# Two layers of windowed attention and MLP: K copied to bf16 before it is spread by parity, PV sums divided block by block

## The chip, the cores and the metric

The kernel runs on one core of a Trainium2 chip. The metric is the time of one execution on the device in microseconds; the median of three runs before the change is 485.0 us.

A core has five engines that run side by side, each in its own program order: TensorE (PE, matmul, with a weight load PEld of its own), VectorE (DVE), ScalarE (ACT), GpSimd (POOL) and SyncE (SP, which issues DMAs here). Matmuls write to PSUM, which has 8 banks; this kernel gives 4 of them to the attention scores (one tile of 4 banks) and 4 single ones to everything else.

## The reference

Two layers, each a windowed attention with 32 heads of 16 and a ReLU MLP, each with a normalization ahead of it and a residual sum behind it. The weights of both layers are the same.

```python
def _A_ref(x, wqkv, wo):                     # x: 1 x 2048 x 512, bf16
    B, S, D = x.shape
    H = 32; Dh = D // H; W = 256
    qkv = (x @ wqkv).reshape(B, S, 3, H, Dh).transpose(2, 0, 3, 1, 4)
    q, k, v = qkv[0], qkv[1], qkv[2]
    scores = jnp.einsum("bhqd,bhkd->bhqk", q, k) * (Dh ** -0.5)
    mask = (idx[:, None] - idx[None, :] >= 0) & (idx[:, None] - idx[None, :] < W)
    p = softmax(where(mask, scores, -1e9))
    o = jnp.einsum("bhqk,bhkd->bhqd", p, v)
    return o.transpose(0, 2, 1, 3).reshape(B, S, D) @ wo

def _B_ref(x, w1, w2):                       # w1: 512 x 1792, w2: 1792 x 512
    return jnp.maximum(x @ w1, 0) @ w2

x = A_x
x = x + _A_ref(layernorm(x), A_wqkv, A_wo);  x = x + _B_ref(layernorm(x), B_w1, B_w2)
x = x + _A_ref(layernorm(x), A_wqkv, A_wo);  x = x + _B_ref(layernorm(x), B_w1, B_w2)
```

## The kernel before

The rows are worked in 8 steps: 2 layers of 4 chunks of 512 rows, called k = 0 to 7. The kernel is written as a graph of small operations, each with the engines it may run on, an assumed time for each, the operations it depends on, and the buffers it takes. While the program is built, a list scheduler in Python plays the graph through with those assumed times and records the instructions of each engine in the order that it finds. On the chip that order is fixed; where an assumed time is off, an engine waits. Where the scheduler sees TensorE idle for 0.4 us, it puts a matmul on an identity there ("warm").

The buffers of the shared kind:

```python
    ps_s = ctx.enter_context(tc.tile_pool(name="ps_s", bufs=1, space=bass.MemoryType.PSUM))  # scores, 4 banks
    psum = Pool("p", 4, ps_d)      # 4 single banks: Q, K, V, PV sums, wo, w1, w2, warm
    xns = Pool("xn", 3, work)
    stg = Pool("stg", 3, work)     # V on its way, and the output rows
    ots = Pool("OT", 3, work)
    EVAC = {512: {"DVE": 0.67, "ACT": 0.59}, 256: {"DVE": 0.42, "ACT": 0.38}}   # assumed times
```

K lies in SBUF twice, once for the even and once for the odd heads of a pair of 16 rows, with the rows of the other parity multiplied by zero (`par` holds 1 or 0 for each partition). It is written by VectorE or ScalarE straight from the PSUM bank of K's matmuls. `KBD` is a ring of 20 slots of 64 keys; a chunk that reaches over the end is written in two pieces for each parity.

```python
    def spread_k(e, layer, c, t, h0, h1, ps):
        ...                                   # pieces a to b of the ring
            for p in range(2):
                o = KBD[:, t, sa:sa + b - a, p, :]
                i = ps[:, 64 * a:64 * b].rearrange("p (s k) -> p s k", k=64)
                if e == "ACT":
                    act.activation(o, i, ACT.Copy, scale=par[:, p:p + 1])
                else:
                    dve.tensor_scalar(out=o, in0=i, scalar1=par[:, p:p + 1], scalar2=None, op0=ALU.mult)
```

```python
        # plan_qkv(k), for each of 4 groups t of 8 heads (chunk 0 in two halves h of 256 rows)
                at = first_slot[units_of[k][t + 4 * (h or 0)]] - wait          # wait = 16 score tiles, 0 in chunk 0
                box, m = group(at, KC, us, kmm, ...)                           # K's matmuls in one bank
                times = {"DVE": 1.46, "ACT": 1.42} if h is None else {"DVE": 0.87, "ACT": 0.83}
                k_done[k, t, h or 0] = op(SOON["qkv"], options(times, lambda e, ...:
                                                      spread_k(e, layer, c, t, h0, h1, box.ps)),
                                          [m, c_par], None, [box])
```

V has such a copy already: it goes from PSUM to a buffer of the pool `stg` (VectorE or ScalarE) and from there to its place (VectorE or GpSimd).

Attention works on units of 8 heads and 512 rows (256 rows in the first and the last chunk). A unit has 5 score tiles (3 in a half unit), 164 in the whole kernel. For each: matmuls to the score banks, exp on ScalarE into one of two buffers Pb, and the triangles of the mask by VectorE (a minimum with `tri`) or GpSimd (selects).

```python
                scores[s] = op(-1e5 + s, {"PE": (...)}, need + ([exps[s - 1]] if s else []))
                exps[s] = op(-1e5, {"ACT": (...)}, [scores[s]] + before)       # before: PV sums of the unit before last
                masks[s].append(op(SOON["mask"], options(times, ...), [exps[s]] + c_tri))
```

Then come the PV sums. Each of 8 heads has 16 columns and one for the sum of the exps (`V2` holds a 1 there). Two blocks of 128 queries go into one bank, one after the other, and are divided together:

```python
            for j0 in range(0, u.nq // 2, 2):
                box = Box(psum)
                prior = None
                for jl in (j0, j0 + 1):
                    ...                        # needs: exps, masks, V of this block
                    for p in range(4):
                        begins = jl == j0 and p == 0
                        def pfn(...):
                            if begins:
                                box.ps = box.tile([P, 2, 4, 2, 17], FP32, "acc")
                            pv_group(u, jl, p, pb, box.ps[:, jl - j0])
                        prior = op(-5e4 + n - (0 if begins else 1000), ...)
                    pvs[n, jl] = prior
                divs[k, u.t, j] = divs[k, u.t, j + 1] = op(
                    SOON["div"], {"DVE": (0.64, dfn)}, [prior] + war + checks[k - 2:k - 1], None, [box])

    def divide(t, j, acc, O, chk):
        sums = acc[:].rearrange("p j a e d -> p j (a e) d")
        rinv = chk[:, j:j + 2, 8 * t:8 * t + 8]
        dve.reciprocal(rinv, sums[:, :, :, 16])
        dve.tensor_tensor(out=O[:, j:j + 2, P * t:P * (t + 1)].rearrange("p j (a d) -> p j a d", d=16),
                          in0=sums[:, :, :, 0:16],
                          in1=rinv.rearrange("p j (a o) -> p j a o", o=1).to_broadcast([P, 2, 8, 16]), op=ALU.mult)
```

When all 4 units have divided a block of O, a DMA transposes it (`OT`); then follow wo, the residual sum, the normalization, w1 with ReLU into `hT`, w2 and the next residual sum. They are filled in between the score tiles of the next chunk. W2 is loaded once the normalized rows of chunk 1 are through (`applied[2]`):

```python
    plan_qkv(0)
    for k in range(NSTEP):
        plan_attention(k)
        if k == 0:
            plan_qkv(1)
            d_w2 = op(0, {"SP": (1.4, lambda: sp.dma_start(w2[:], ...), 9.0)}, applied[2])
        plan_rest(k)
        if 0 < k < NSTEP - 1:
            plan_qkv(k + 1)
```

Almost all instructions are recorded through one helper in line 106, so the profile gives that line for them; they are told apart by the names of their tiles.

Of the kernel before, what the change touches and what calls it, by code (L numbers as in the profile page):

```python
# [9 lines left out]
FP32 = mybir.dt.float32  # L10
BF16 = mybir.dt.bfloat16
I32 = mybir.dt.int32
AX = mybir.AxisListType
ACT = mybir.ActivationFunctionType
ALU = mybir.AluOpType
P = 128
# [46 lines left out]
def kernel(  # L63
# [51 lines left out]
    pe, dve, act, pool, sp = (InOrder(x) for x in (nc.tensor, nc.vector, nc.scalar, nc.gpsimd, nc.sync))  # L115
# [38 lines left out]
    par = const.tile([P, 2], FP32, name="par")  # L154
# [66 lines left out]
    def op(key, opts, deps=(), take=None, uses=(), keep=0):  # L221
        uses = list(uses) + ([take] if take is not None and take not in uses else [])
        return Op(key, opts, deps, take, uses, keep)
# [15 lines left out]
    d_wo, d_w1 = landed(18.0), landed(24.0)  # L239


    def copy(e, o, i, relu=False):
        if e == "ACT":
            act.activation(o, i, ACT.Relu if relu else ACT.Copy)
        elif e == "POOL":
            pool.tensor_copy(o, i)
        elif relu:
            dve.tensor_relu(o, i)
        else:
            dve.tensor_copy(o, i)  # L250
# [3 lines left out]
    def options(times, fn):  # L254
        return {e: (t, lambda e=e: fn(e)) for e, t in times.items()}
# [67 lines left out]
    def spread_k(e, layer, c, t, h0, h1, ps):  # L323
        s0 = slot(layer, 8 * c)
        for a, b in ([(h0, h1)] if s0 + h1 <= NSLOT or s0 + h0 >= NSLOT else [(h0, NSLOT - s0), (NSLOT - s0, h1)]):
            sa = (s0 + a) % NSLOT
# [3 lines that stand above are left out]
                if e == "ACT":  # L330
                    act.activation(o, i, ACT.Copy, scale=par[:, p:p + 1])
                else:
                    dve.tensor_scalar(out=o, in0=i, scalar1=par[:, p:p + 1], scalar2=None, op0=ALU.mult)

    def spread_v(e, layer, c, j, src):
        v4 = src.rearrange("p (a e d) -> p e a d", e=2, d=16)
# [44 lines left out]
    def seen(u, jl):  # L381
        return [kb for kb in range(2 * jl - 4, 2 * jl + 2) if u.c > 0 or kb + u.q0 >= 0]

    def pv_group(u, jl, p, pb, acc):
        kbs = seen(u, jl)
        for i, kb in enumerate(kbs):
            g, lo, at = u.place[kb]
            col = (4 * g + p) * PW + 64 + 64 * (at + 2 * jl - lo)
            mm(acc[:, p], Pb[pb][:, col:col + P], V2[:, slot(u.k // NCH, 8 * u.c + u.q0 + kb), :, 4 * u.t + p, :],
               i == 0, i == len(kbs) - 1)  # L390

    def divide(t, j, acc, O, chk):

        sums = acc[:].rearrange("p j a e d -> p j (a e) d")
        rinv = chk[:, j:j + 2, 8 * t:8 * t + 8]
        dve.reciprocal(rinv, sums[:, :, :, 16])
        dve.tensor_tensor(out=O[:, j:j + 2, P * t:P * (t + 1)].rearrange("p j (a d) -> p j a d", d=16),
                          in0=sums[:, :, :, 0:16],
                          in1=rinv.rearrange("p j (a o) -> p j a o", o=1).to_broadcast([P, 2, 8, 16]), op=ALU.mult)

    def accumulate_check(chk, first):
        mx = small.tile([P, 1], FP32, name="chk_mx")
# [60 lines left out]
    def plan_qkv(k):  # L463
# [24 lines left out]
        for h in range(2) if k == 0 else (None,):  # L488
            cols = slice(0, 512) if h is None else slice(256 * h, 256 * h + 256)
            h0, h1 = (0, 8) if h is None else (4 * h, 4 * h + 4)  # L490
            us = 0.216 if h is None else 0.115
            need_x = dst if h is None else dst[2 * h:2 * h + 2]
            w = 512 if h is None else 256
            for t in range(4):
                at = first_slot[units_of[k][t + 4 * (h or 0)]] - wait
                idx = 4 * k + t

                def kmm(kc, ps, t=t, cols=cols):
                    mm(ps[:, cols], wqkv[:, kc, D + t * P:D + (t + 1) * P], xnT[0][:, kc, cols], kc == 0, kc == KC - 1)
                box, m = group(at, KC, us, kmm, need_x + [d_w[1]] + old[len(old) * t // 4:len(old) * (t + 1) // 4], lead=1000)  # L500
                times = {"DVE": 1.46, "ACT": 1.42} if h is None else {"DVE": 0.87, "ACT": 0.83}
                k_done[k, t, h or 0] = op(SOON["qkv"], options(times, lambda e, t=t, h0=h0, h1=h1, box=box:
                                                      spread_k(e, layer, c, t, h0, h1, box.ps)),
                                          [m, c_par], None, [box])

                def qmm(kc, ps, t=t, cols=cols):
                    mm(ps[:, cols], wqkv[:, kc, t * P:(t + 1) * P], xnT[0][:, kc, cols], kc == 0, kc == KC - 1)
                last_use = [scores[s] for n, u in enumerate(units) if 4 * u.k + u.t == idx - 7
                            for s in range(first_slot[n], first_slot[n] + len(u.groups))]
                box, m2 = group(at + 0.1, KC, us, qmm, need_x + [d_w[0]] + last_use, lead=1000)  # L510

                def qev(e, t=t, cols=cols, box=box, idx=idx):
                    q = first(Q, (k, t), lambda: work.tile([P, 512], BF16, name="Qt", tag=f"Q{idx % 7}", bufs=1))
                    copy(e, q[:, cols], box.ps[:, cols])
                q_done[k, t, h or 0] = op(SOON["qkv"], options(EVAC[w], qev), [m2], None, [box])
                mine += [m, m2]
# [16 lines left out]
    def plan_attention(k):  # L533
        layer, c = divmod(k, NCH)
        prev = units_of.get(k - 1, []) if c else []
        for n in units_of[k]:
# [3 lines left out]
            for g in range(len(u.groups)):  # L540
# [17 lines left out]
                for m in u.masks(g):  # L558
                    times = {"DVE": 0.32 + 0.14 * (len(m) - 1), "POOL": 0.93 * len(m)}
                    masks[s].append(op(SOON["mask"], options(times, lambda e, m=m, g=g, pb=pb: mask(e, m, places(pb, g))), [exps[s]] + c_tri))  # L560
            for j0 in range(0, u.nq // 2, 2):
                box = Box(psum)
                prior = None
                for jl in (j0, j0 + 1):
                    kbs = seen(u, jl)
                    need = [prior]
                    for g in sorted({u.place[kb][0] for kb in kbs}):
                        need += [exps[first_slot[n] + g]] + masks[first_slot[n] + g]
                    for kb in kbs:
                        b = u.q0 + kb  # L570
                        need.append(v_done[k, b // 2] if b >= 0 else v_done[k - 1, (b + 8) // 2])
                    for p in range(4):
                        begins = jl == j0 and p == 0

                        def pfn(u=u, jl=jl, j0=j0, pb=pb, box=box, p=p, begins=begins):
                            if begins:
                                box.ps = box.tile([P, 2, 4, 2, 17], FP32, "acc")
                            pv_group(u, jl, p, pb, box.ps[:, jl - j0])
                        prior = op(-5e4 + n - (0 if begins else 1000),
                                   {"PE": (0.025 * len(kbs) + (0.03 if p == 0 else 0.0), pfn)},  # L580
                                   need if p == 0 else [prior], box if begins else None, [box])
                    pvs[n, jl] = prior
                j = u.q0 // 2 + j0

                def dfn(u=u, j=j, box=box):
                    o = first(O_of, u.k, lambda: work.tile([P, 4, D], BF16, name="O", tag="O", bufs=1))
                    divide(u.t, j, box.ps, o, chks[u.k % 2])
                war = [turned[k - 1, i] for i in range(4)] if k else []
                divs[k, u.t, j] = divs[k, u.t, j + 1] = op(
                    SOON["div"], {"DVE": (0.64, dfn)}, [prior] + war + checks[k - 2:k - 1], None, [box])  # L590
        checks.append(op(40, {"DVE": (1.1, lambda k=k: accumulate_check(chks[k % 2], k == 0))},
                         [divs[k, t, j] for t in range(4) for j in range(4)] + checks[-1:]))

# [124 lines left out]
        push(t, None, None)  # L718
    started, score_end, idle_since, log = set(), [0.0], [1.9], []
    score_next = [0]  # L720

    by_name = {"PE": pe, "ACT": act, "DVE": dve, "POOL": pool, "SP": sp}

    def choose(e, t):
        best = None
# [153 lines left out]
    with tc.If(flag > 0):  # L879
# [13 lines left out]
        for layer in range(2):  # L893
            for c in range(NCH):
# [3 lines left out]
                for t in range(4):  # L898
                    q = work.tile([P, 512], BF16, name="Qt", tag=f"Q{t}", bufs=1)
                    Qts.append(q)  # L900
                    whole(KC, lambda kc, ps: mm(ps[:], wqkv[:, kc, t * P:(t + 1) * P], xnT[:, kc, :], kc == 0, kc == KC - 1),
                          lambda ps: nc.vector.tensor_copy(q[:], ps[:]))
                    whole(KC, lambda kc, ps: mm(ps[:], wqkv[:, kc, D + t * P:D + (t + 1) * P], xnT[:, kc, :], kc == 0, kc == KC - 1),
                          lambda ps: spread_k("DVE", layer, c, t, 0, 8, ps))
                for j in range(4):
                    whole(KC, lambda kc, ps: mm(ps[:], xnT[:, kc, j * P:(j + 1) * P], wqkv[:, kc, 2 * D:3 * D], kc == 0, kc == KC - 1),
                          lambda ps: spread_v("DVE", layer, c, j, ps[:]))
# [52 lines left out]
```

## Time and profile before

| | before |
|---|---|
| median of three runs | 485.0 us (483.33 to 486.06) |
| span of the profiled execution | 484.1 us |
| first exp begins, last exp ends | 12.7 us, 427.6 us |
| TensorE busy | 464.2 us |
| VectorE busy | 358.1 us |
| ScalarE busy | 338.9 us |
| GpSimd busy | 302.2 us |
| granted TensorE clock | 0.999 |

A busy share is an average over the span. Matmuls overlap in the records, so a matmul's own duration is longer than the distance from one to the next, and TensorE is never as full as its busy time says. The idle time of an engine is put down to what ended it. A group of instructions gives the work's tiles as out<-in, then partitions x elements and types, the number of instructions, busy time, mean duration in ns, and the idle time ahead of them.

### The profile page before, as it was taken

To read this page: it belongs to the slowest core of one execution; us is meant where nothing else is said; L and a number is where in the kernel's file an instruction comes from. 1 tells how busy PE (TensorE), PEld (TensorE's weight loads), DVE (VectorE), ACT (ScalarE), POOL (GpSimd) and SP (SyncE) were. 2 spreads that over 40 slices of the span, in tenths; PEclk is the share of its full clock that TensorE was granted. 3 is DMA by queue.
4 is the path that set the end of the run, shared out by engine and by line. 5 is a ranking of instruction groups with operands and counts; after the bars stand their busy time and mean duration, and the time that the engine had idled before them with its cause. 6 is when DMAs were issued, how large, how long until landed. Compare 5 with 4: busy or idle time off the path is not lost.

```text
span 484.1 us, 14517 instructions
## 1 busy us (share of the span) xinstructions
PE 464.2 (96%) x6061; PEld 249.1 (51%) x6061; DVE 358.1 (74%) x850; ACT 338.9 (70%) x283; POOL 302.2 (62%) x677
## 2 busy tenths in 40 slices
PE   7979999998999989999999999999999999999995
PEld 3545656654545544555544555545546355554662
DVE  6989978867986689967978868997658878363111
ACT  3767878876878767777779877878766667754440
POOL 7778887647775778856867766777754547531000
PEclk9999999999999999999999999999999999999999
DMA  8790311003300051002211122020242002100000
GB/s 265 249 193 15 60 30 25 2 3 61 67 7 3 18 84 34 4 1 45 58 34 24 24 44 45 2 46 3 44 79 45 12 1 47 34 12 12 33 23 28
DMA packets 54649, 21.98 MB, mean 45 GB/s; under 512 B 46128, under 2 KB 54064, under 8 KB 54576
## 3 DMA queue, kind: packets, MB, share of 16 engines
q1 hardware_dynamic: 54576, 20.98, 19.6%
q8 instruction: 49, 0.80, 0.7%
q14 instruction: 24, 0.20, 0.2%
HBM read 7.86 MB, written 2.10 MB: 21 GB/s over the span
## 4 chain that ended last, share of the span: by engine, by line
PE 79%; DVE 6%; DMA 6%; POOL 4%; ACT 2%; issue 2%; POOLq 0%; ACTq 0%; DVEq 0%
PE ps_d L106 56%; PE acc L106 14%; PE Sps L106 9%; DMA OT<-O 5%; POOL Pb L106 2%; ACT Pb L106 2%; DVE KBD L106 1%; POOL xn L106 1%; DVE st L106 1%; DMA xnT<-xn 1%; POOL rstds L106 1%; DVE V2f L106 1%; DVE Vst L106 1%; DVE Pb L106 1%; DMA x_sb<-in_A_x_dram 1%
## 5 line engine op out<-in xcount | busy, mean ns | idle before, releaser
L106 ACT ACTIVATE Pb<-Sps 128x2048 bf16<-128x2048 f32 (+4 forms) x164 | 283.9, 1731 | 94.2 <-PE Sps L106 75.3
L106 POOL TENSOR_SCALAR_AFFINE_SELECT Pb<-Pb 64x256 bf16<-64x256 bf16 x492 | 214.2, 435 | 106.5 <-ACT Pb L106 86.3
L106 PE MATMUL ps_d<-xn2T,w 128*128 128x512 bf16 (+1 forms) x560 | 109.8, 337 | 0.6 <-DVE hT L106 0.4
L106 PE MATMUL ps_d<-w,hT 128*128 128x512 bf16 x448 | 109.9, 380 | 0.0
L106 PEld LDWEIGHTS <-Pb 128*128 128x128 bf16 x2880 | 83.8, 96 | 22.2 <-issue 7.9
L106 PE MATMUL acc<-V2f,Pb 128*128 128x34 bf16 x2880 | 89.9, 178 | 0.7 <-POOL Pb L106 0.6
L106 DVE TENSOR_TENSOR Pb<-Pb,tri 128x512 bf16<-128x512 bf16 (+1 forms) x144 | 62.6, 441 | 13.4 <-ACT Pb L106 12.3
L106 PEld LDWEIGHTS <-w 128*128 128x128 bf16 x560 | 50.7, 97 | 39.0 <-issue 4.8
L106 PE MATMUL ps_d<-xnT,wqkv 128*128 128x512 bf16 (+1 forms) x288 | 67.0, 356 | 1.9 <-ACT KBD L106 0.9
L106 PE MATMUL Sps<-Qt,KBD 32*128 32x192 bf16 (+4 forms) x1536 | 62.3, 249 | 3.4 <-ACT Pb L106 2.9
L106 PEld LDWEIGHTS <-hT 128*128 128x128 bf16 x448 | 40.1, 97 | 44.5 <-issue 3.0
L106 DVE TENSOR_SCALAR hT<-ps_d 128x512 bf16<-128x512 f32 (+1 forms) x72 | 44.6, 625 | 13.8 <-PE ps_d L106 13.5
L106 PEld LDWEIGHTS <-KBD 32*128 32x128 bf16 x1536 | 25.5, 92 | 54.0 <-issue 49.7
L106 ACT ACTIVATE hT<-ps_d 128x256 bf16<-128x256 f32 (+1 forms) x68 | 32.0, 473 | 24.4 <-PE ps_d L106 22.6
L106 DVE TENSOR_SCALAR KBD<-ps_d,par 128x256 bf16<-128x256 f32 (+1 forms) x80 | 44.1, 603 | 2.2 <-PE ps_d L106 2.1
L106 DVE BATCH_NORM_STATS2 st<-x_sb 128x6 f32<-128x512 f32 (+1 forms) x64 | 43.8, 684 | 1.4 <-DMA x_sb<-in_A_x_dram 0.7
L106 DVE TENSOR_TENSOR x_sb<-ps_d,x_sb 128x512 f32<-128x512 f32 x48 | 32.4, 682 | 15.9 <-PE ps_d L106 15.3
L106 PEld LDWEIGHTS <-wqkv 128*128 128x128 bf16 x288 | 25.6, 97 | 26.8 <-issue 5.2
L106 PE MATMUL ps_d<-wo,OT 128*128 128x512 bf16 x128 | 33.8, 380 | 4.1 <-DMA OT<-O 4.0
L106 DVE TENSOR_TENSOR ob<-ps_d,x_sb 128x512 bf16<-128x512 f32 x16 | 11.0, 688 | 33.1 <-PE ps_d L106 33.1
L106 PE MATMUL ps_d<-wqkv,xnT 128*128 128x512 bf16 x128 | 34.0, 380 | 0.4 <-DVE Vst L106 0.3
L106 POOL TENSOR_TENSOR rstds<-rstds,mhalf 128x2 f32<-128x2 f32 (+1 forms) x33 | 23.7, 718 | 16.5 <-DVE rstds L106 14.7
(55 smaller groups left out, 287.5 us busy)
## 6 DMA issues: line engine op xcount, KB each, us to landing
w<-in_B_w_dram SPq DMA_DIRECT2D x2, 1792.0 KB, 11.0
out_dram<-ob SPq DMA_DIRECT2D x16, 128.0 KB, 1.7
wqkv<-in_A_wqkv_dram SPq DMA_DIRECT2D x3, 512.0 KB, 6.6
x_sb<-in_A_x_dram SPq DMA_DIRECT2D x3, 512.0 KB, 9.0
x_sb<-in_A_x_dram SPq DMA_DIRECT2D x2, 256.0 KB, 3.0
wo<-in_A_wo_dram SPq DMA_DIRECT2D x1, 512.0 KB, 8.9
xnT<-xn SPq DMA_TRANSPOSE x28, 2.5
OT<-O SPq DMA_TRANSPOSE x28, 2.5
```

The source lines that it names most:

```text
L106: inst = fn(*a, **k)
```

## The change

From chunk 1 on, K goes from PSUM to a bf16 buffer of the pool `stg` by one copy (VectorE or ScalarE), which sets the PSUM bank free, and is spread by parity from that buffer by VectorE or GpSimd. Chunk 0 keeps the spread from PSUM. And each block of 128 queries has its PV sums in a bank of its own and is divided by itself, where two shared a bank and a division. The load of W2 is placed the same in both.

```diff
@@ spread_k
-                    dve.tensor_scalar(out=o, in0=i, scalar1=par[:, p:p + 1], scalar2=None, op0=ALU.mult)
+                    by_name[e].tensor_scalar(out=o, in0=i, scalar1=par[:, p:p + 1], scalar2=None, op0=ALU.mult)
@@ divide
-        sums = acc[:].rearrange("p j a e d -> p j (a e) d")
-        rinv = chk[:, j:j + 2, 8 * t:8 * t + 8]
-        dve.reciprocal(rinv, sums[:, :, :, 16])
-        dve.tensor_tensor(out=O[:, j:j + 2, P * t:P * (t + 1)].rearrange("p j (a d) -> p j a d", d=16),
-                          in0=sums[:, :, :, 0:16],
-                          in1=rinv.rearrange("p j (a o) -> p j a o", o=1).to_broadcast([P, 2, 8, 16]), op=ALU.mult)
+        rinv = chk[:, j, 8 * t:8 * t + 8].rearrange("p (a e) -> p a e", e=2)
+        dve.reciprocal(rinv, acc[:, :, :, 16])
+        dve.tensor_tensor(out=O[:, j, P * t:P * (t + 1)].rearrange("p (a e d) -> p a e d", a=4, e=2),
+                          in0=acc[:, :, :, 0:16],
+                          in1=rinv.rearrange("p a (e o) -> p a e o", o=1).to_broadcast([P, 4, 2, 16]), op=ALU.mult)
@@ plan_qkv
-                k_done[k, t, h or 0] = op(SOON["qkv"], options(times, lambda e, t=t, h0=h0, h1=h1, box=box:
-                                                      spread_k(e, layer, c, t, h0, h1, box.ps)),
-                                          [m, c_par], None, [box])
+                if k == 0:
+                    k_done[k, t, h or 0] = op(...)                 # as before
+                else:
+                    ks = Box(stg)
+
+                    def kev(e, box=box, ks=ks):
+                        ks.t = ks.tile([P, 512], BF16, "Kst")
+                        copy(e, ks.t[:], box.ps[:])
+                    ev = op(SOON["qkv"], options(EVAC[512], kev), [m], ks, [box, ks])
+                    k_done[k, t, 0] = op(SOON["qkv"], options({"DVE": 0.8, "POOL": 1.3}, lambda e, t=t, ks=ks:
+                                                              spread_k(e, layer, c, t, 0, 8, ks.t[:])),
+                                         [ev, c_par], None, [ks])
@@ plan_attention
-            for j0 in range(0, u.nq // 2, 2):
-                ...                                                # two blocks in one bank
+            for jl in range(u.nq // 2):
+                kbs = seen(u, jl)
+                ...                                                # the same needs, for this block alone
+                box = Box(psum)
+                prior = None
+                for p in range(4):
+                    def pfn(u=u, jl=jl, pb=pb, box=box, p=p):
+                        if p == 0:
+                            box.ps = box.tile([P, 4, 2, 17], FP32, "acc")
+                        pv_group(u, jl, p, pb, box.ps)
+                    prior = op(-5e4 + n - (1000 if p else 0), {"PE": (0.025 * len(kbs) + (0.03 if p == 0 else 0.0), pfn)},
+                               [prior] if p else need, None if p else box, [box])
+                pvs[n, jl] = prior
...
-                divs[k, u.t, j] = divs[k, u.t, j + 1] = op(
-                    SOON["div"], {"DVE": (0.64, dfn)}, [prior] + war + checks[k - 2:k - 1], None, [box])
+                divs[k, u.t, j] = op(SOON["div"], {"DVE": (0.5, dfn)}, [pvs[n, jl]] + war + checks[k - 2:k - 1], None, [box])
```

As the scheduler plays the whole graph through anew, the order of most instructions moves, and which engine takes a copy, a mask or a V spread moves with it.

More of the change, by code (lines that the diff above doesn't have):

```diff
@@ L239 @@
     d_wo, d_w1 = landed(18.0), landed(24.0)
+    by_name = {"PE": pe, "ACT": act, "DVE": dve, "POOL": pool, "SP": sp}
     def copy(e, o, i, relu=False):
@@ L501, in plan_qkv @@
                 times = {"DVE": 1.46, "ACT": 1.42} if h is None else {"DVE": 0.87, "ACT": 0.83}
-                k_done[k, t, h or 0] = op(SOON["qkv"], options(times, lambda e, t=t, h0=h0, h1=h1, box=box:
-                                                      spread_k(e, layer, c, t, h0, h1, box.ps)),
-                                          [m, c_par], None, [box])
+                if k == 0:
+                    k_done[k, t, h or 0] = op(SOON["qkv"], options(times, lambda e, t=t, h0=h0, h1=h1, box=box:
+                                                                   spread_k(e, layer, c, t, h0, h1, box.ps[:])),
+                                              [m, c_par], None, [box])
+                else:
[7 more added lines that the diff above has]
+                                         [ev, c_par], None, [ks])
                 def qmm(kc, ps, t=t, cols=cols):
@@ L560, in plan_attention @@
                     masks[s].append(op(SOON["mask"], options(times, lambda e, m=m, g=g, pb=pb: mask(e, m, places(pb, g))), [exps[s]] + c_tri))
-            for j0 in range(0, u.nq // 2, 2):
+            for jl in range(u.nq // 2):
+                kbs = seen(u, jl)
+                need = []
+                for g in sorted({u.place[kb][0] for kb in kbs}):
+                    need += [exps[first_slot[n] + g]] + masks[first_slot[n] + g]
+                for kb in kbs:
+                    b = u.q0 + kb
+                    need.append(v_done[k, b // 2] if b >= 0 else v_done[k - 1, (b + 8) // 2])
+                j = u.q0 // 2 + jl
@@ L562, in plan_attention @@
                 box = Box(psum)
                 prior = None
[L564 to L582, printed above, removed]
@@ L583, in plan_attention @@
-                j = u.q0 // 2 + j0
+                for p in range(4):
[5 more added lines that the diff above has]
+                               [prior] if p else need, None if p else box, [box])
@@ L720 @@
     score_next = [0]
-    by_name = {"PE": pe, "ACT": act, "DVE": dve, "POOL": pool, "SP": sp}
     def choose(e, t):
@@ L903 @@
                     whole(KC, lambda kc, ps: mm(ps[:], wqkv[:, kc, D + t * P:D + (t + 1) * P], xnT[:, kc, :], kc == 0, kc == KC - 1),
-                          lambda ps: spread_k("DVE", layer, c, t, 0, 8, ps))
+                          lambda ps: spread_k("DVE", layer, c, t, 0, 8, ps[:]))
                 for j in range(4):
```

## The prediction

> **What bounds the kernel now.** I read the page's busy table and chain first, then the groups of instructions by shape, the waits, and a stretch of the timeline. The busy table and the shares of the chain:
>
> ```profile
> PE 464.2 (96%) x6061; PEld 249.1 (51%) x6061; DVE 358.1 (74%) x850; ACT 338.9 (70%) x283; POOL 302.2 (62%) x677
> ...
> PE 79%; DVE 6%; DMA 6%; POOL 4%; ACT 2%; issue 2%; POOLq 0%; ACTq 0%; DVEq 0%
> ```
>
> TensorE looks full and the chain runs through it. But the timeline of two steps of attention (columns: start, length, engine, work, idle time before) says more:
>
> ```profile
> 101.84 2.33 PE L106 MATMUL ps_d<-w,hT 128*128 128x512 bf16 x10
> 102.02 1.88 ACT L106 ACTIVATE Pb<-Sps 128x2048 bf16<-128x2048 f32 x1 [0.71 <-PE Sps L106]
> ...
> 104.11 0.26 PEld L106 LDWEIGHTS <-KBD 32*128 32x128 bf16 x12 [0.42 <-issue]
> 104.11 0.40 PE L106 MATMUL Sps<-Qt,KBD 32*128 32x320 bf16 x12
> ...
> 104.61 1.88 ACT L106 ACTIVATE Pb<-Sps 128x2048 bf16<-128x2048 f32 x1 [0.71 <-PE Sps L106]
> ```
>
> One score tile (four PSUM banks, one buffer) goes to and fro: exp 1.88 us, then 0.71 us until the next scores are there, 2.59 us a step (102.02 to 104.61). TensorE fills a step with other matmuls and then waits for the exp: ten 512-column matmuls run from 101.84 to 104.17, about 0.217 us apart ((2.33 - 0.38) / 9), and the scores start at 104.11, 0.2 us after the exp ended at 103.90. So two things are in balance: the loop of 164 score tiles and exps, and a TensorE program laid out to just fill it. By shape:
>
> ```profile
> L106 ACT ACTIVATE Pb<-Sps 128x2048 bf16<-128x2048 f32 x132 | 247.8, 1877 | 77.2 <-PE Sps L106 62.5 <-POOL Pb L106 4.4 <-DVE mvs L106 2.7
> L106 DVE TENSOR_TENSOR O<-acc,chk 128x256 bf16<-128x256 f32 x64 | 27.2, 424 | 2.2
> L106 DVE RECIPROCAL chk<-acc 128x16 f32<-128x16 f32 x64 | 16.1, 252 | 21.8 <-PE acc L106 21.4
> L106 DVE TENSOR_SCALAR KBD<-ps_d,par 128x512 bf16<-128x512 f32 x38 | 26.6, 742 | 1.4 <-PE ps_d L106 1.3
> L106 DVE TENSOR_SCALAR KBD<-ps_d,par 128x256 bf16<-128x256 f32 x42 | 17.5, 476 | 0.8 <-PE ps_d L106 0.7
> ```
>
> All exps take 283.9 us; with 163 gaps of 0.71 us that is 400 us, and first exp to last is 427.6 - 12.7 = 415. So only about 15 us of the loop is anything else, ahead of it lie 12.7 us and behind it 56. TensorE's waits, in total, times, longest:
>
> ```profile
> PE ps_d L106 <- DMA OT<-O: 4.0, 6, 1.6
> PE Sps L106 <- ACT Pb L106: 2.9, 7, 0.8
> ...
> PE ps_d L106 <- ACT KBD L106: 0.9, 1, 0.9
> ...
> PE warm L106 <- DVE KBD L106: 0.2, 1, 0.2
> ```
>
> The K spread holds TensorE up for about 1 us in all. The transposes of O are the largest wait, and it is 4 us.
>
> **What the skill says.** The Trainium skill, "VectorE: DVE Perf Modes", section "The perf-mode tier table": single-source operations on 16-bit data in SBUF run in a faster mode than those with a PSUM operand. The trace agrees: the normalization of a bf16 row (128x512, same kind of operation) takes 383 ns at the least, the K spread from PSUM 742. "SBUF — State Buffer", section "SBUF: two separate sides": VectorE in its two-port modes and GpSimd exclude each other from a shared port pair for a whole instruction. The normalizations on VectorE go from 383 to 857 ns; that fits, but the trace doesn't name the cause. "PSUM — Partial Sum Buffer", section "The four PSUM rules": GpSimd can't read PSUM, which is why K must be copied before GpSimd can spread it; no GpSimd instruction here touches PSUM. "Perfetto Trace Analysis", section "Identifying the Most-Contended Engine": matmul busy time is a bad measure, as matmuls are pipelined; here a matmul counts 0.38 us where they start 0.217 apart.
>
> **The change, part by part.** The instruction streams of both programs can be counted, engine by engine.
>
> *PV sums and division.* Before, 64 pairs at 252 + 424 = 676 ns: 43.3 us of VectorE. After, 128 single blocks. An element costs (742 - 476) / 256 = 1.04 ns, so the division of 128 elements is 424 - 133 = 291 ns; the reciprocal of 8 I put at 220. That makes 128 x 0.511 = 65.4 us, 22 more. In return a bank is held for one block's sums.
>
> *K.* In chunks 1 to 7 there are 28 tiles. Before, 26 were spread by VectorE: 19 in 2 pieces of 742 and 7, wrapped around the ring of slots, in 4 pieces of 476: 41.5 us (2 on ScalarE). After, 13 copies on VectorE at 682 ns (as the Vst copies) and 15 on ScalarE at 594; 20 tiles spread by VectorE, 16 in 2 pieces of about 383 and 4 in 4 of about 250, 16.3 us; 8 on GpSimd (8 pieces of 768 and 16 of about 430: 13 us). VectorE: 8.9 + 16.3 - 41.5 = -16 us. A PSUM bank is let go after 0.6 to 0.7 us in place of 1.5. The time until K is ready hardly changes: 0.68 + 0.77 against 1.48; by GpSimd it is 0.6 + 1.5, with more than ten steps in hand in most chunks.
>
> *What the layout moves with it.* On VectorE: 4 more Q copies, 8 fewer V copies, 16 more V spreads, 5 more hT; with division and K +10 us, so 368 of 484 (76%). ScalarE: +6 us (K copies and 8 V copies against fewer Q, hT and K spreads), 345. GpSimd: 20 more selects (+8.7), K (+13), 16 fewer V spreads (-6.8), 2 fewer normalizations (-2.5), 315 (65%). None becomes full.
>
> *W2.* The load stands where it stood, behind the normalizations of chunk 1, in both: no effect.
>
> *TensorE.* The same matmuls, except that the layout puts in 35 warming matmuls in place of 44: 9 x 0.217 = 2.0 us less. I counted the work between each score tile and the next at 0.217 us a 512-column matmul and 0.0255 a PV matmul. Ahead of the first score tile it is 7.3 us in both, behind the last 51.6 in both, between them 331.7 before and 329.8 after. A step holds about 2.15 us beside its scores without delaying the next exp; what lies above that sums to 11.4 us before and 10.3 after. That is -1.1 us. All else of the layout's gain lies under the exps.
>
> *Waits.* O of the first block of a pair is ready one block's sums earlier (24 PV matmuls, 0.7 us), and its transpose can start ahead of the other's. The last block's can't. Of 4 us I give 1. Against that, VectorE has 10 us more of short work in a fixed order, and each late operation pushes a mask or a hT copy that TensorE or the next exp waits for: I give back 0.6.
>
> Sum: -1.1 - 1.0 + 0.6 = -1.5 us, from 485.0 to 483.5.
>
> **Rivals.** (a) *VectorE becomes the bound in the first 80 us.* It is busy 69 of the first 80 us there, chunk 0 and 1 are spread and normalized, and 16 more divisions cost 16 x 0.511 - 8 x 0.676 = 2.8 us in each chunk. K of chunk 1 takes part of it back. If it all shows twice, and port exclusion stretches the K pieces, 489 to 491. Against it: TensorE has warming matmuls there, so there is room. (b) *PSUM banks were the hidden limit.* Four banks serve all matmuls but the scores; shorter holds would then take away most of the odd gaps between exps (some 15 us, of which 5 to 6 are a planned block of matmuls) and the time falls to 476 to 478. Against it: the waits name the bank's readers (hT, Vst) for less than 1 us, and most of TensorE's idle time lies at the two ends. (c) *The fixed order drifts.* A GpSimd spread here costs 1.54 us where the layout assumes 1.3, plus exclusion by VectorE; a mask behind it comes late and PV and the next exp with it (the GpSimd masks already end 4.4 us of exp waits). 486 to 489. (d) *Nothing at all:* the loop of exps is untouched in its 2.59 us a step: 485.
>
> **Range and chances.** The loop and the work behind it, 7 + 415 + 56, are the same program; only the gaps move. The three times before spread over 2.7 us, so 2 us is near what can be seen. (b) sets the low end at 477, (a) and (c) the high end at 490. For over 2% it must be below 475.3, which needs most odd gaps gone: 3%. Above 494.7 needs both (a) and (c): 4%. Within 2%: 93%.
>
> **What would show it.** Right: exps at 1.88 us with 0.71 between them in most steps; 35 warming matmuls; VectorE near 368 us; division pieces near 290 ns; K pieces from SBUF near 383 ns; the work behind the last exp about 56 us; transposes of O waited for less than 4 us. Wrong: K pieces on VectorE or GpSimd stretched far over 0.4 and 0.8 us, waits for the division or for KBD above 2 us, new gaps between exps of several microseconds, or TensorE's waits gone in chunks 1 to 6.

## The result and the profile after

The changed kernel takes 492.6 us (median of 4 runs, 491.66 to 493.6) against 485.3 for the kernel before (its three runs and one more): a ratio of 1.0157, 95% interval 1.0121 to 1.0194. It is slower, by less than 2%, and outside the range of 477 to 490 that was predicted.

The busy table and the shares of the chain, after:

```profile
PE 463.9 (95%) x6052; PEld 249.8 (51%) x6052; DVE 365.4 (75%) x992; ACT 343.9 (70%) x290; POOL 328.8 (67%) x699
...
PE 70%; POOL 15%; DMA 5%; DVE 4%; ACT 3%; issue 3%; POOLq 0%; ACTq 0%; DVEq 0%
```

Before, GpSimd had 4% of the chain and TensorE 79%. No engine became full: GpSimd is at 67%. But it now stands in the chain that ended last for 15% of the span. The rows that answer to those shown before (exps, division, and K's spread, which now comes from the copy Kst), after:

```profile
L106 ACT ACTIVATE Pb<-Sps 128x2048 bf16<-128x2048 f32 x132 | 247.8, 1877 | 82.7 <-PE Sps L106 67.6 <-POOL Pb L106 3.8 <-DVE Pb L106 3.4
L106 DVE TENSOR_TENSOR O<-acc,chk 128x128 bf16<-128x128 f32 x128 | 37.3, 291 | 4.4
L106 DVE RECIPROCAL chk<-acc 128x8 f32<-128x8 f32 x128 | 25.8, 202 | 21.5 <-PE acc L106 19.1
...
L106 POOL TENSOR_SCALAR KBD<-Kst,par 128x256 bf16<-128x256 bf16 x16 | 15.5, 988 | 0.1
L106 DVE TENSOR_SCALAR KBD<-Kst,par 128x512 bf16<-128x512 bf16 x32 | 14.1, 480 | 0.1
L106 POOL TENSOR_SCALAR KBD<-Kst,par 128x512 bf16<-128x512 bf16 x8 | 13.3, 1676 | 0.3
```

The exps take the same 1877 ns, the division the predicted 291. What stands out is GpSimd: a K piece of 512 takes 1676 ns, where the prediction had 768, and one of 256 takes 988, where it had 430. All 24 pieces make 28.8 us, where it had 13, and the layout (the scheduler's plan) 10.4 (8 tiles at 1.3). The pieces of 512 belong to one tile at 33.5 us, two at 51.7 and one at 324.7; the pieces of 256 belong to tiles that wrap around the ring, at 84, 117, 380 and 391 us.

When the exps start shows where the time goes (the first is number 0). Number 16 starts at 49.2 us (before: 49.7), number 24 at 74.8 (before: 68.7), number 120 at 315.6 (before: 310.1), and the last one ends at 433.9 (before: 427.6). So against the kernel before, some 6 us are lost between 49 and 75 us, and as much is still missing at the end. In that stretch the timeline of the changed kernel reads (start, length, engine, work, idle time before and what ended it):

```profile
51.75 6.47 POOL L106 TENSOR_SCALAR KBD<-Kst,par 128x512 bf16<-128x512 bf16 x4
...
58.18 0.72 POOL L106 TENSOR_TENSOR rstds<-rstds,mhalf 128x2 f32<-128x2 f32 x1
...
61.66 0.72 POOL L106 TENSOR_TENSOR rstds<-rstds,mhalf 128x2 f32<-128x2 f32 x1
62.34 4.60 POOL L106 TENSOR_SCALAR_AFFINE_SELECT Pb<-Pb 64x256 bf16<-64x256 bf16 x10
62.42 0.96 DVE L106 TENSOR_SCALAR xn<-x_sb,mvs,rstds 128x512 bf16<-128x512 bf16 x2 [5.30 <-POOL rstds L106]
63.30 1.93 DVE L106 TENSOR_SCALAR hT<-ps_d 128x256 bf16<-128x256 f32 x5
63.75 1.01 PE L106 MATMUL ps_d<-xn2T,w 128*128 128x256 bf16 x4 [4.37 <-DVE hT L106]
...
66.27 1.88 ACT L106 ACTIVATE Pb<-Sps 128x2048 bf16<-128x2048 f32 x1 [5.89 <-PE Sps L106]
```

Read it from the top. Two tiles of K take GpSimd 6.47 us. Behind them in its order stand the roots for the next normalizations (`rstds`), with two normalizations on GpSimd between the first root and the second. VectorE has a normalization in its order that needs the second root, and waits 5.30 us for it. Behind that on VectorE stand five copies of hT, which free the PSUM banks, and TensorE waits 4.37 us for the first. Behind that stand the next scores, and the exp waits 5.89 us. None of these waits is for K itself: this is one late stretch of GpSimd, handed on through three fixed orders.

### The profile page after: what moved, and what is told of

It reads as the page before. It is cut to its first block, busy times and chain, and to the rows that moved or that the text cites. A ratio compares the mean times of both kernels' runs of the same rounds, so it can differ in the third digit from the quotient of the medians.

```text
span 489.6 us, 14698 instructions
## 1 busy us (share of the span) xinstructions
PE 463.9 (95%) x6052; PEld 249.8 (51%) x6052; DVE 365.4 (75%) x992; ACT 343.9 (70%) x290; POOL 328.8 (67%) x699
## 4 chain that ended last, share of the span: by engine, by line
PE 70%; POOL 15%; DMA 5%; DVE 4%; ACT 3%; issue 3%; POOLq 0%; ACTq 0%; DVEq 0%
PE ps_d L106 51%; PE acc L106 11%; PE Sps L106 8%; POOL Pb L106 7%; DMA OT<-O 4%; POOL KBD L106 3%; ACT Pb L106 3%; POOL V2f L106 1%; POOL xn L106 1%; POOL rstds L106 1%; DVE V2f L106 1%; POOL nbs L106 1%; DMA x_sb<-in_A_x_dram 1%; DMA xnT<-xn 1%; DVE st L106 1%
## 5 line engine op out<-in xcount | busy, mean ns | idle before, releaser
L106 POOL TENSOR_SCALAR_AFFINE_SELECT Pb<-Pb 64x256 bf16<-64x256 bf16 x512 | 222.0, 434 | 91.2 <-ACT Pb L106 69.6
L106 PEld LDWEIGHTS <-Pb 128*128 128x128 bf16 x2880 | 84.2, 96 | 28.8 <-issue 9.3
L106 PE MATMUL acc<-V2f,Pb 128*128 128x34 bf16 x2880 | 91.1, 178 | 4.7 <-POOL Pb L106 3.1
L106 DVE TENSOR_TENSOR Pb<-Pb,tri 128x512 bf16<-128x512 bf16 (+1 forms) x143 | 59.2, 421 | 10.2 <-ACT Pb L106 9.8
L106 DVE TENSOR_SCALAR hT<-ps_d 128x512 bf16<-128x512 f32 (+1 forms) x77 | 47.0, 615 | 10.8 <-PE ps_d L106 10.0
L106 ACT ACTIVATE hT<-ps_d 128x256 bf16<-128x256 f32 (+1 forms) x63 | 30.0, 478 | 23.0 <-PE ps_d L106 21.3
L106 DVE RECIPROCAL chk<-acc 128x8 f32<-128x8 f32 x128 | 25.8, 202 | 21.5 <-PE acc L106 19.1
L106 DVE TENSOR_TENSOR O<-acc,chk 128x128 bf16<-128x128 f32 x128 | 37.3, 291 | 4.4
```

The costliest lines, as they stand in the source:

```text
L106: inst = fn(*a, **k)
```

## The experiments

Two theories were there beside the late GpSimd (A): that 128 single divisions load VectorE too much (B), and that VectorE's and GpSimd's K pieces shut each other out (C). Ratios are to the kernel before, run beside them on the same chip.

**K on VectorE alone.**

```diff
-  options({"DVE": 0.8, "POOL": 1.3}, ... spread_k(e, layer, c, t, 0, 8, ks.t[:]))
+  options({"DVE": 0.8}, ... spread_k(e, layer, c, t, 0, 8, ks.t[:]))
```

> The whole change, but the spread of the K copy may run on VectorE alone. Theory A (a GpSimd piece takes 1.68 us where the layout assumes 0.65, and all that stands behind it on GpSimd comes late): the 5.9 us gap between exps near 66 us is gone, time 484 to 487 us. Theory B (128 single divisions load VectorE too much): 491 to 494 us, since they stay. Theory C (VectorE's K pieces from SBUF and GpSimd shut each other out): 491 us or more, since 28 tiles go to VectorE in place of 20.

Measured: 482.5 us, ratio 0.9944 (0.9923 to 0.9965). Faster than both kernels, and below the range of A. The exp in question starts at 60.7 us after a gap of 1.29. This speaks against B and C as the cause of the loss: all single divisions are in it, and VectorE spreads all 28 tiles. But the layout is another one too; the run in the same order, below, is the one that leaves no such doubt.

**PV sums by block alone**, K spread from PSUM as before (the K part of the diff left out).

> Only the PV part of the change: blocks divided singly, K spread from PSUM as before. Theory A: 483 to 486 us. Theory B: 490 us or more. Theory C: 483 to 486 us.

Measured: 484.9 us, 0.9982 (0.997 to 0.9993). The single divisions don't cost time; they gain about 1 us.

**The K part alone**, PV sums in pairs (the PV part of the diff left out).

> Only the K part: K copied and spread from the copy on VectorE or GpSimd (6 tiles fall to GpSimd), PV sums in pairs as before. Theory A: 487 to 492 us, depending on what stands behind the GpSimd pieces; each piece of 512 at 1.6 to 1.7 us. Theory B: 484 to 486 us. Theory C: 488 to 492 us.

Measured: 494.7 us, 1.0178 (1.014 to 1.0217), somewhat more than A's upper end. GpSimd's 18 pieces have a median of 936 ns and reach 1802. The exps lose 4.8 us up to number 24 (6.1 in the whole change) and 4 more near 250 us, where TensorE waits 2.79 us for a transpose of normalized rows. What made that transpose late was not followed up.

**The GpSimd piece by itself.** The changed kernel with 21 more instructions behind GpSimd's last one, while VectorE has little to do (busy 4.3 of those 25 us), on data no longer used. `three` issues a form three times and a small fill behind them; `wide` is 8 runs of 64 columns, `flat` one run of 512:

```diff
+    three(out=wide, in0=mi3, scalar1=par[:, 0:1], scalar2=None, op0=ALU.mult)                         # 1: K's form, strided
+    three(out=flat, in0=mi, scalar1=par[:, 0:1], scalar2=None, op0=ALU.mult)                          # 2: contiguous
+    three(out=flat, in0=mi, scalar1=1.0, scalar2=None, op0=ALU.mult)                                  # 3: constant
+    three(out=wide, in0=mi3, scalar1=par[:, 0:1], scalar2=par[:, 1:2], op0=ALU.mult, op1=ALU.add)     # 4: two operations, strided
+    three(out=flat, in0=mi, scalar1=par[:, 0:1], scalar2=par[:, 1:2], op0=ALU.mult, op1=ALU.add)      # 5: two, contiguous
+    three(out=wide, in0=mi3, scalar1=par[:, 0:1], scalar2=0.0, op0=ALU.mult, op1=ALU.add)             # 6: two, the second a constant
+    for _ in range(3): pool.tensor_copy(wide, mi3)                                                    # 7: copy
```

> The changed kernel with 21 GpSimd instructions of 128x512 bf16 behind its last one, three of each form, while VectorE has little to do. In order: multiply by a pointer scalar into a strided output (8 runs of 64, as K's); the same into a contiguous output; multiply by a constant, contiguous; multiply and add with two pointer scalars, strided; the same contiguous (as a normalization); multiply by pointer and add of constant 0, strided; a copy, strided. If the strides make K's piece slow: the strided ones take 1.6 us and the contiguous ones 0.77. If the form with one operation does: the first three take 1.6 us, the others 0.77 us. If shared ports with VectorE do: all take 0.77 us here.

GpSimd's timeline of that kernel, the seven forms in this order (start, length of three together; small fills of 0.1 us between them are left out):

```profile
446.09 5.19 POOL L106 TENSOR_SCALAR Pb<-Pb,par 128x512 bf16<-128x512 bf16 x3
...
451.38 5.05 POOL L106 TENSOR_SCALAR Pb<-Pb,par 128x512 bf16<-128x512 bf16 x3
...
456.52 4.64 POOL L106 TENSOR_SCALAR Pb<-Pb 128x512 bf16<-128x512 bf16 x3
...
461.27 2.50 POOL L106 TENSOR_SCALAR Pb<-Pb,par 128x512 bf16<-128x512 bf16 x3
...
463.88 2.50 POOL L106 TENSOR_SCALAR Pb<-Pb,par 128x512 bf16<-128x512 bf16 x3
...
466.48 2.26 POOL L106 TENSOR_SCALAR Pb<-Pb,par 128x512 bf16<-128x512 bf16 x3
...
468.80 1.95 POOL L106 COPY Pb<-Pb 128x512 bf16<-128x512 bf16 x3
```

A third of each: 1.73, 1.68 and 1.55 us with one operation; 0.83, 0.83 and 0.75 with two; 0.65 for a copy. So the form decides, and the stride does nothing (4 and 5 are equal, 1 and 2 differ by 3%). A multiply followed by an add of zero takes less than half the time of the multiply alone. The slow form is as slow here as in the kernel (1676 ns), though VectorE has little to do: it is busy for 0.69 of the 5.3 us of form 1, and for the same 0.69 of the 2.65 us of form 4, which is fast. So shared ports are not the cause. Why the one-operation form is slower no run shows.

**The same order, with the fast form.** Every instruction stands where it stood in the changed kernel, and computes the same; only the form of GpSimd's 24 pieces differs. The two traces show the same operations on the same tiles in the same order on each engine.

```diff
-                    by_name[e].tensor_scalar(out=o, in0=i, scalar1=par[:, p:p + 1], scalar2=None, op0=ALU.mult)
+                    by_name[e].tensor_scalar(out=o, in0=i, scalar1=par[:, p:p + 1], scalar2=0.0 if e == "POOL" else None,
+                                             op0=ALU.mult, **({"op1": ALU.add} if e == "POOL" else {}))
```

> The changed kernel with every instruction where it stood on its engine; only GpSimd's K pieces are written with a second operation (multiply by par, add 0.0), which took 0.75 us in place of 1.7. If the slow form of these 24 instructions is the whole cause: the gap between exps near 66 us shrinks to about 1.3 us or less and the time is 482 to 485 us, below the kernel before. If the layout itself (single divisions, other order) costs: 488 us or more.

Measured: 485.2 us, 0.9981 (0.9968 to 0.9995), at the upper edge of what was expected. The loss is gone: the ratio falls by 1.76 percentage points (1.0157 to 0.9981; the medians differ by 7.4 us), and only 24 instructions were changed. This settles the cause, as nothing else differs: single divisions and VectorE's K pieces are all still there. The same pieces and the same copies of hT, in the timeline of this kernel:

```profile
50.27 2.69 POOL L106 TENSOR_SCALAR KBD<-Kst,par 128x512 bf16<-128x512 bf16 x4
52.92 0.72 POOL L106 TENSOR_TENSOR rstds<-rstds,mhalf 128x2 f32<-128x2 f32 x1
...
57.31 0.96 DVE L106 TENSOR_SCALAR xn<-x_sb,mvs,rstds 128x512 bf16<-128x512 bf16 x2 [1.61 <-POOL rstds L106]
...
58.66 0.60 PE L106 MATMUL ps_d<-xn2T,w 128*128 128x256 bf16 x4 [0.99 <-DVE hT L106]
...
60.76 1.88 ACT L106 ACTIVATE Pb<-Sps 128x2048 bf16<-128x2048 f32 x1 [2.10 <-PE Sps L106]
```

6.47 us became 2.69, VectorE's wait 5.30 became 1.61, TensorE's 4.37 became 0.99, the exp's 5.89 became 2.10: 3.8, 3.7, 3.4 and 3.8 us less. The exp's wait did not shrink to the 1.3 us expected. Such figures of one profile are rough: the kernel with the 21 instructions, the same as the changed one up to 445 us, has 4.01 us where the changed one has 5.89. A longer stretch is steadier: from exp number 16 to number 24 it takes 25.6 us in the changed kernel and 25.0 in that one, 20.8 here and 18.9 in the kernel before.

There is a second, smaller loss, from exp number 124 to 128: 13.3 us in the changed kernel, 11.5 in this one. In the changed kernel and then in this one:

```profile
324.67 3.35 POOL L106 TENSOR_SCALAR KBD<-Kst,par 128x512 bf16<-128x512 bf16 x2
...
334.54 0.63 PE L106 MATMUL acc<-V2f,Pb 128*128 128x34 bf16 x19 [0.72 <-POOL V2f L106]
...
336.71 1.88 ACT L106 ACTIVATE Pb<-Sps 128x2048 bf16<-128x2048 f32 x1 [2.50 <-PE Sps L106]
```

```profile
320.92 1.35 POOL L106 TENSOR_SCALAR KBD<-Kst,par 128x512 bf16<-128x512 bf16 x2
...
331.16 1.88 ACT L106 ACTIVATE Pb<-Sps 128x2048 bf16<-128x2048 f32 x1 [0.69 <-PE Sps L106]
```

Behind the one tile of K, GpSimd copies V late, the PV sums wait for it, and the next exp starts after a gap of 2.50 us in place of 0.69.

The ratio is 0.37 points above that of K on VectorE, so this order loses elsewhere: the gap ahead of exp number 44 is 4.90 us here and 1.95 there. In it TensorE waits for a transpose of O, for 1.19 us in the kernel before. In the changed kernel and then in this one:

```profile
126.09 1.90 PE L106 MATMUL ps_d<-wo,OT 128*128 128x512 bf16 x8 [2.73 <-DMA OT<-O]
```

```profile
120.43 3.34 PE L106 MATMUL ps_d<-wo,OT 128*128 128x512 bf16 x8 [2.92 <-DMA OT<-O]
```

The order has the wait with either form. The same eight matmuls take 1.4 us longer here, because the granted TensorE clock is at half from 120.7 to 124.1 us, and the gap grows from 3.09 to 4.90. The changed kernel has such a stretch of 3.41 us too, from 63.6 to 67.1 us, right where TensorE's wait of 4.37 us ends. The kernel before and K on VectorE have none until their last microsecond, and no wait of TensorE over 1.9 us. So a part of what the late GpSimd costs is probably a lower clock behind the wait; but no run here tests what sets such a stretch off, and behind the wait of 2.73 us above there is none.

**The fast form in the pieces of 512 alone.** As the last, but only for the 8 pieces of 512 (`two = e == "POOL" and b - a == 8`). The expectation is wrong on where they stand: six are before 60 us and two at 325; of the 16 pieces of 256, eight are from 84 to 121 us and eight from 380 to 395.

> As the run before, but only the 8 GpSimd pieces of 512 elements (all before 60 us) get the second operation; the 16 pieces of 256 after 300 us stay at about 0.99 us. If the one event near 52 to 66 us is most of the loss: 484 to 487 us. If late pieces cost as much: 488 us or more.

Measured: 485.6 us, 0.9996 (0.998 to 1.0011). Of the 1.76 points, 1.61 come from the 8 pieces of 512, the two events above; how much each of the two brings to the time was not separated. The 16 pieces of 256, 15.5 us of GpSimd, cost nothing that these intervals can tell, though a tile of four of them takes 4.0 us where the plan has 1.3.

**The slow form, but in the plan.**

```diff
-  options({"DVE": 0.8, "POOL": 1.3}, ...
+  options({"DVE": 0.8, "POOL": 3.5}, ...
```

> The changed kernel with the slow GpSimd pieces as they are, but the layout told 3.5 us for a tile on GpSimd in place of 1.3; it still gives GpSimd 6 tiles. If the loss comes from the plan not knowing (work behind the pieces comes late): 484 to 487 us, though the slow instructions are still there. If the slow pieces cost by their mere length: 489 us or more.

Measured: 487.9 us, 1.0032 (1.0013 to 1.005), between the two expectations. GpSimd still gets 6 slow tiles, yet 1.25 of the 1.57 points are back. So slow tiles need not cost much where the plan knows of them. But the plan also gives GpSimd two tiles fewer, and one before 60 us in place of three, so this run doesn't separate a known length from a better place; a part of the loss stays, which another order could also bring.

**The fast form, in the plan** (1.7 us for a tile on GpSimd):

> GpSimd's K pieces with the second operation, and the layout told 1.7 us for a tile on GpSimd in place of 1.3, so that plan and chip agree (5 tiles go to GpSimd). If drift from the plan is what costs: 481 to 484 us. If GpSimd is a bad place for K at any length: above the 482.5 us of K on VectorE by 2 us or more.

Measured: 482.7 us, 0.9933 (0.9908 to 0.9958), like K on VectorE alone, and below the same form unknown to the plan (0.9981). So GpSimd is no bad place for K here.

**K on VectorE alone, PV sums in pairs:**

> Only the K part, and on VectorE alone; PV sums in pairs as before. If the earlier release of the PSUM bank by the K copy is what brings the gain of the whole change with K on VectorE (482.5 us): 482 to 484 us. If it takes both parts: 484 to 486 us.

Measured: 485.0 us, 0.9985 (0.9967 to 1.0003). So neither part alone gives the 0.9944 that both give. The PV part is worth about 0.2%; the K part measures the same, but its interval takes in no gain at all. Why both together bring more is not settled: the layout is made anew each time.

**The plan with measured times.** Fast form, K 0.95 us on VectorE and 1.7 on GpSimd, masks on VectorE 0.36 and 0.13 more, division 0.52.

```diff
-  options({"DVE": 0.8, "POOL": 1.3}, ...
+  options({"DVE": 0.95, "POOL": 1.7}, ...
-  times = {"DVE": 0.32 + 0.14 * (len(m) - 1), ...
+  times = {"DVE": 0.36 + 0.13 * (len(m) - 1), ...
-  SOON["div"], {"DVE": (0.5, dfn)}
+  SOON["div"], {"DVE": (0.52, dfn)}
```

> GpSimd pieces with the second operation, and the assumed times set to what was measured: K on VectorE 0.95, on GpSimd 1.7, masks on VectorE 0.36 and 0.13 more for the second, division 0.52. If more truth in the plan brings more: 480 to 482 us. If the plan is as good as it gets with the K time right: 482 to 484 us, as the run with 1.7 alone.

Measured: 480.6 us, 0.9892 (0.9849 to 0.9935). It beats both kernels and is the fastest of all here; from the run with 1.7 alone its interval is not apart.

## Why the prediction was wrong

- *The bound* was read rightly: exps at 1877 ns before and after, 55.7 us behind the last exp (about 56 predicted), 35 warming matmuls. (The sum "7 + 415 + 56" in the range should have 12.7 us ahead of the first exp; the 7.3 us are TensorE's work there.)
- *PV sums and division* were right: 291 ns as worked out, the reciprocal 202 for 220. VectorE rose by 7.3 us for 10. That it would not become the bound held too; the PV part alone is 0.2% faster.
- *K* is the step that failed, in the term "8 on GpSimd (8 pieces of 768 and 16 of about 430: 13 us)". The 768 came from the row of GpSimd's normalizations, a multiply and an add; K's piece is a multiply alone, 1676 and 988 ns, 28.8 us in all, and GpSimd is busy for 328.8 us where 315 were predicted. The row was taken by operation name and shape, and the number of operations in it was not compared. VectorE's pieces, put at 383, took 480.
- *From busy time to time.* "None becomes full" was true and beside the point. The tile took 3.4 us where the plan had 1.3 (4.0 where it wraps around the ring), and what mattered was which instructions stood behind it. "More than ten steps in hand" looked at who waits for K; those who waited were behind K on GpSimd, not K's readers. Two of its signs of being wrong came true: GpSimd's pieces stretched far over 0.8 us, and a new gap of several microseconds between exps.
- *Rival (c), drift,* had the mechanism and even the engine, but with 1.54 against 1.3 us for a tile and a cost of 1 to 4 us. The true difference is 2.1 us for a tile in two pieces. It pointed to a mask behind the K pieces; in the trace it was a root of the normalization, and later a copy of V. With the fast form the same order is 0.9 us faster than the kernel before (ratio 0.9981), where the prediction had 1.5. That the rest of the sum is so near is in part luck, as the next point shows.
- *Waits for O.* One microsecond less was promised; TensorE's waits for these transposes went from 4.0 to 4.7 us, and are 5.6 in the same order with the fast form.

## What to carry to other kernels

Where the order of instructions is fixed ahead by assumed times, one wrong time costs by what stands behind it in its queue, not by its share of the engine: here eight pieces cost nearly all of the loss, and sixteen others, just as wrongly timed, nothing that could be measured. So compare each new instruction's assumed time with a measured one of exactly its form, number of operations included, before asking whether its engine has room. And when a change loses, keep the order and alter only the suspect's duration: that settled here in one run what layouts made anew could only suggest.

## What the hardware showed that was not expected

On GpSimd, a 128x512 bf16 multiply by a scalar took 1.55 to 1.73 us as the only operation, with strided and with contiguous output. With a second scalar added it took 0.83 us, strided or contiguous, and with an added zero 0.75 (0.69 in the changed kernel's order). On VectorE, the 128x512 piece of K from SBUF took 480 ns on average in the changed kernel, 334 the shortest and 703 the longest. And in the middle of the program the granted TensorE clock was at half for 3.41 us at a time, in these profiles only in kernels where TensorE had a wait of over 2 us (the changed kernel, the K part alone, the same order with the fast form).
